# Fewer small GpSimd instructions per batch, and the two-product gate in every tile of batches 1 to 7

## The chip, the cores and the metric

The kernel runs on one core of a Trainium2 chip. A core has TensorE (PE: matmuls, with the weight loads PEld beside them), VectorE (DVE), ScalarE (ACT), GpSimd (POOL) and SyncE (SP, which here only issues transfers). Each engine works through its own queue of instructions in the order in which the program lists them. The metric is the device time of one execution in microseconds (us); lower is better.

## The reference

```python
def _attn_ref(x):                      # x: [8, 3008, 256]
    X = np.fft.fft(x, axis=1)
    X = np.fft.fft(X, axis=2)
    return X.real.astype(np.float32)

def _moe_ref(x, w_gate, w_val, w_out): # [24064, 256], [256, 1536] twice, [1536, 256]
    gate = np.maximum(x @ w_gate, 0.0)
    val = x @ w_val
    return (gate * val @ w_out).astype(np.float32)
```

The real part of a 2-D Fourier transform over sequence and channels of each of the 8 batches goes, row by row, through a gated layer with ReLU.

## The kernel before

**Transform.** Per batch, GpSimd *folds* x: it adds rows and channels to their mirror images, so that the transform over the sequence becomes products of TensorE with cosine and sine tables, and the transform over the channels is multiplied into the gate and value weights beforehand (`WA`, `WB`, and `WM`, the sine weight with the sign for the mirrored row). The folds of a batch are a list made by `fold_steps(b)`:

- six `fold_a` (L113), then the same for channel 0 in three small instructions (`fold_a0`, L116);
- `channel_128`: two small sums `c128p` (L148), and eight small scalings into `FN` (L151), the operand of the Nyquist channel;
- `load_rows` of the next batch, issued by SP;
- six `fold_pq` (L121), then `small`: six `fold_pq0` for channel 0 (L124);
- gathers of the next batch's mirrored rows (`load_mirror`, L102), interleaved with the folds into F (L128, and L132 for channel 0) and G (L137), families 1 and 0.

**Order.** The program is written out by hand. From batch 1 on, a batch is 3 blocks ("thirds") of 12 feature tiles, 36 *slots*. A slot (`slot`) lists the value products of tile k, the gate of tile k+2, the second (mirrored) half of tile k-1, a share of the output products of the block before (L496), and then some steps of other work: transform products of the next batch, 3 of them in the slots that `DFT_EVEN` and `DFT_ODD` name, and fold steps of the batch after that. Batch b transforms batch b+1 and folds batch b+2; batches 6 and 7 fold nothing. In odd batches the Nyquist products (`nyquist_steps`, L443) of two batches come after slot 18; they read `FN`, with batch b+2's part of it.

Fold steps are given out by a credit. Each step has a declared cost in us, the first number of its pair:

```python
def run_fold(us):
    credit = credit + us if todo_fold else 0
    while todo_fold and credit >= todo_fold[0][0]:
        cost, step = todo_fold.pop(0)
        step()
        credit -= cost
...
run_fold(fold_us * (1.6 if not new else .9))   # in slot; fold_us is 1.1 in batch 1, .9 after
```

`new` says that the slot builds the gate of a tile of the new kind. What is left at a batch's end is issued there at once (`run_fold(99)`). Six steps of batch 2's folds are left over for batch 1.

**Tiles.** A tile is 504 (or 497) columns of one of 12 features, with a plus and a mirrored half.

- An *old* tile (kind "o") takes its gate in three products: WA and WB, ReLU by ScalarE (L585), then WM on top and ReLU again; VectorE multiplies each by the value (L593).
- A *new* tile (kind "n") takes it in two: ScalarE seeds the bank (L684), WM gives the sine part q (L689), which ScalarE copies out (L692), WA adds the cosine part (L696). VectorE makes one argument, p - q/2 (L700, in `both`), **GpSimd adds q for the other (L701)**, and VectorE does ReLU and the multiplication in one instruction for each half (L597).

The value takes three products either way (L570, L571, L575). The L701 of tile k is listed in slot k-2 and its mult in slot k+1. In batches 1 to 5, 18 tiles are old: 6 in batch 1 and 3 in each of 2 to 5; the rest of batches 1 to 7, 234 tiles, are new. Batch 0 has another form (`first_tile`, `single_tile`), with narrower segments.

Of the kernel before, what the change touches and what calls it, by code (L numbers as in the profile page):

```python
# [13 lines left out]
ALU = mybir.AluOpType  # L14
# [18 lines left out]
def kernel(  # L33
# [8 lines left out]
    nc = tc.nc  # L42
# [18 lines left out]
    def single(name, shape, dt=F32, pool=const):  # L61
        return pool.tile(shape, dt, name=name, tag=name)
# [13 lines left out]
    XD = single("XD", [128, 2, 3, 2, D])  # L76
    XG = single("XG", [128, 2, 3, 2, D])
    PQ = single("PQ", [128, 2, 3, 2, D])

    FF = [single(f"F{i}", [128, 2, 3, 2, 129], BF16) for i in range(2)]  # L80
    GG = [single(f"G{i}", [128, 2, 3, 2, 128], BF16) for i in range(2)]
    FN = single("FN", [128, 2, 3, 2, B // 2, 2, 2], BF16)
# [6 lines left out]
    def load_rows(b, queue=None):  # L89
        o = b * S * D  # L90
        for t in range(3):
            for r in range(2):
                n = (128, 128, 120)[t]
                (queue if queue and r and t < 2 else nc.sync).dma_start(out=XD[0:n, r, t],
                                                                         in_=dram(x, o + (1 + r * H + t * 256) * D, [[2 * D, n], [D, 2], [1, D]]))

        for r in range(2):
            nc.sync.dma_start(out=XD[120:121, r, 2], in_=dram(x, o + r * H * D, [[0, 1], [0, 2], [1, D]]))

    def load_mirror(b, t, r):  # L100
        n = (128, 128, 121)[t]
        nc.gpsimd.indirect_dma_start(  # L102
            out=XG[0:n, r, t, :, :].rearrange("p a d -> p (a d)"), out_offset=None, in_=pairs,
            in_offset=bass.IndirectOffsetOnAxis(ap=gidx[0:n, 2 * t + r:2 * t + r + 1] if t < 2 else gidx2[0:n, r:r + 1], axis=0),
            element_offset=b * S * D)

    def flat(ap):
        return ap.rearrange("p t q d -> p (t q) d")
# [3 lines left out]
    def fold_a(e, p, r, t):  # L112
        e.tensor_tensor(XG[p, r, t, ::-1, 1:D], XG[p, r, t, ::-1, 1:D], XD[p, r, t, :, D - 1:0:-1], op=ALU.add)  # L113

    def fold_a0(e, p, t):
        e.tensor_tensor(XG[p, :, t, ::-1, 0], XG[p, :, t, ::-1, 0], XD[p, :, t, :, 0], op=ALU.add)  # L116

    SIGN = (ALU.add, ALU.subtract)

    def fold_pq(e, p, i, t):  # L120
        e.tensor_tensor(PQ[p, i, t, :, 1:D], XG[p, 0, t, ::-1, D - 1:0:-1], XG[p, 1, t, ::-1, 1:D], op=SIGN[i])  # L121

    def fold_pq0(e, p, i, t):
        e.tensor_tensor(PQ[p, i, t, :, 0], XG[p, 0, t, ::-1, 0], XG[p, 1, t, ::-1, 0], op=SIGN[i])  # L124

    def fold_f(e, p, ts, fam, b):
        s = flat(PQ[p, fam, ts])
        e.tensor_tensor(flat(FF[b % 2][p, fam, ts])[:, :, 1:129], s[:, :, 1:129], s[:, :, D - 1:D - 129:-1], op=ALU.add)  # L128

    def fold_f0(e, p, ts, fam, b):  # L130
        s = flat(PQ[p, fam, ts])[:, :, 0:1]
        e.tensor_tensor(flat(FF[b % 2][p, fam, ts])[:, :, 0:1], s, s, op=ALU.add)  # L132

    def fold_g(e, p, ts, fam, b):

        s = flat(PQ[p, 1 - fam, ts])
        e.tensor_tensor(flat(GG[b % 2][p, 1 - fam, ts])[:, :, 1:128], s[:, :, 1:128], s[:, :, D - 1:D - 128:-1], op=ALU.subtract)  # L137

    def fold_steps(b):

        e, p, ts = nc.gpsimd, slice(0, 128), slice(0, 3)
        steps = [(1.1, lambda r=r, t=t: fold_a(e, p, r, t)) for t in range(3) for r in range(2)]
        steps += [(0.5, lambda: [fold_a0(e, p, t) for t in range(3)])]

        def channel_128():
            for i in range(2):
                c = c128p[:, i]
                e.tensor_tensor(c, XG[:, 0, :, ::-1, 128], XG[:, 1, :, ::-1, 128], op=SIGN[i])  # L148
                for par in range(2):
                    for half in range(2):  # L150
                        e.tensor_scalar(FN[:, i, :, par, b // 2, half, b % 2], c[:, :, par], scalar1=-2.0 if par == 0 and half == i else 2.0,  # L151
                                        op0=ALU.mult, scalar2=0.0, op1=ALU.add)
        steps.append((0.5, channel_128))
        gathers = []
        if b + 1 < B:
            steps.append((0.0, lambda: load_rows(b + 1)))
            gathers = [(1.3, lambda r=r, t=t: load_mirror(b + 1, t, r)) for t in range(3) for r in range(2)]
        steps += [(1.1, lambda i=i, t=t: fold_pq(e, p, i, t)) for t in range(3) for i in range(2)]

        def small():  # L160
            for i in range(2):
                for t in range(3):
                    fold_pq0(e, p, i, t)
        steps.append((0.8, small))
        last = []
        for fam in (1, 0):
            last.append((1.7, lambda fam=fam: fold_f(e, p, ts, fam, b)))
            last.append((1.9, lambda fam=fam: (fold_f0(e, p, ts, fam, b), fold_g(e, p, ts, fam, b))))
        for k in range(6):
            steps += gathers[k:k + 1] + last[k:k + 1]  # L170
        return steps
# [3 lines left out]
    def iota(dst, pattern, base, mult):  # L175
        nc.gpsimd.iota(dst, pattern=pattern, base=base, channel_multiplier=mult, allow_small_or_imprecise_dtypes=True)
# [16 lines left out]
    dvec = single("dvec", [128, 129], pool=st_)  # L193
    go = single("go", [128, 2])
    c128p = single("c128p", [128, 2, 3, 2])

    iota(gidx[:].rearrange("p (t r) -> p t r", r=2), [[-128, 2], [-H // 2, 2]], H - 1, -1)
    iota(pidx[:], [[0, 1]], 0, 1)
# [9 lines left out]
    for r, want in enumerate((0, H // 2)):  # L208
        have = H - 1 - 256 - 120 - r * H // 2
        nc.vector.scalar_tensor_tensor(gf[:, r:r + 1], in0=z[:], scalar=float(want - have), in1=gf[:, r:r + 1],  # L210
                                       op0=ALU.mult, op1=ALU.add)
# [48 lines left out]
    for n, c in enumerate(order):  # L260
        q, m = (single(f"{s}{c}", [128, NJ], pool=st_) for s in "qm")
# [41 lines left out]
    for t in range(3):  # L303
        p, ts = slice(0, ROWS[1][t]), slice(t, t + 1)
# [12 lines left out]
    for p, ts in ((slice(0, 128), slice(0, 2)), (slice(0, ROWS[1][2]), slice(2, 3))):  # L317
        for part in (fold_f, fold_f0, fold_g):
            part(nc.gpsimd, p, ts, 0, 0)
    iota(kvec[:, 0:NE], [[2, NE]], 0, 0)  # L320
    start_pool.__exit__(None, None, None)
    ch128 = nc.dram_tensor("ch128", (B, 4 * NJ + 1), BF16, kind="Internal").ap()
    b2 = single("b2", [128, NF])
# [292 lines left out]
    def tile_of(block, fi, uvc):  # L616
        c0, n = block[:2]
        cols = slice(c0, c0 + n)
        return {"n": n, "fi": fi, "f": slice(fi * 128, (fi + 1) * 128), "us": uvc[0][:, cols], "vs": uvc[1][:, cols], "c": uvc[2][:, cols]}
# [45 lines left out]
    def new_tiles():  # L665
        for b in range(1, B):
            for blk, block in enumerate(thirds):
                for fi in range(NF):
                    st = tile_of(block, fi, uv[b])
                    st["kind"] = "o" if b < 6 and fi % (6 if b < 2 else 12) == 5 else "n"  # L670
                    yield st

    def prime():
# [5 lines left out]
    def seed(st, p=None):  # L679

        if st is None or st["kind"] == "o":
            return
        st["p"] = p or bank("p")
        nc.scalar.activation(st["p"][:, 0:st["n"]], st["c"], ACTF.Copy, scale=b2[:, st["fi"]:st["fi"] + 1])  # L684

    def sine_part(st):
        n = st["n"]
        st["g"] = bank("g")
        nc.tensor.matmul(st["g"][:, 0:n], lhsT=WM[0][:, st["f"]], rhs=st["vs"], start=True, stop=True)  # L689
        q = space()  # L690
        st["s"] = q, space(), q
        nc.scalar.copy(q[:, 0:n], st["g"][:, 0:n])  # L692

    def cosine_part(st):
        n = st["n"]
        nc.tensor.matmul(st["p"][:, 0:n], lhsT=WA[0][:, st["f"]], rhs=st["us"], start=False, stop=True, skip_group_check=True)  # L696

    def both(st):
        n, (q, sp, sm) = st["n"], st["s"]
        nc.vector.scalar_tensor_tensor(sp[:, 0:n], in0=q[:, 0:n], scalar=-0.5, in1=st["p"][:, 0:n], op0=ALU.mult, op1=ALU.add)  # L700
        nc.gpsimd.tensor_tensor(sm[:, 0:n], sp[:, 0:n], q[:, 0:n], op=ALU.add)  # L701
# [40 lines left out]

    uv = {0: (U, V, CB)}
    tiles, ahead = new_tiles(), []

    for b in range(B):
        blocks = thirds if b else segments
        more_b = {} if b else more
        if 0 < b < B - 2:
            todo_fold += fold_steps(b + 2)  # L750
        for blk, block in enumerate(blocks):
# [3 lines left out]
            if b == 0 and blk > 1:  # L755
                todo_fold = fold_steps(blk - 1)
                later = todo_fold[-6:] if blk == 3 else []
                del todo_fold[len(todo_fold) - len(later):]
                run_fold(99)
                todo_fold = later  # L760
            if blk == (0 if b else 2) and b + 1 < B:
# [4 lines left out]
                steps, todo_dft = todo_dft, []  # L766
# [20 lines left out]
            if (b, blk) == (0, 0):  # L787
                for fi in range(NF):
                    st = tile_of(block, fi, (U, V, CB))
# [4 lines left out]
            elif not paired:  # L794
                for fi in range(NF):
                    st = tile_of(block, fi, (U, V, CB))
                    add_h(st, hs)
                    tag = {(3, 8): "g", (3, 9): "d", (3, 10): "g", (3, 11): "d"}.get((blk, fi), "p")
                    last = []
                    if (blk, fi) == (3, 11):  # L800
                        last = [lambda: (sine_part(ahead[1]), cosine_part(ahead[1]), both(ahead[1]), seed(ahead[2]))]
# [54 lines left out]
```

## Time and profile before

| What | Value |
|---|---|
| median of 3 runs | 647.6 us (647.58 to 647.83) |
| profiled execution: span, first to last instruction | 646.1 us |
| what the median has beyond the span | 1.5 us |
| busy: PE / DVE / ACT / POOL | 96% / 84% / 70% / 83% |
| granted TensorE clock | 1.00 |
| batch 1 from, to | 114.0, 189.4 us |
| batches 2 to 5, each | 74.2 to 75.3 us |
| batch 6 | 73.6 us |
| POOL L701, 504 columns | 1.25 us each, 234 of them |
| POOL small instructions (L116, L124, L132, L148, L151) | 0.20 to 0.23 us each |

A row of a group names line, engine, operation and operands, then busy time, mean duration and the idle time ahead. A stretch row gives the busy microseconds of PE, PEld, DVE, ACT and POOL with the number of instructions, then the granted clock, the DMA share and GB/s. A waits row says who waited for whom, the total, the number of times and the longest. The chain of waits is followed back from the end of its window: at each step to what released an instruction, or to the one before it on its engine. A batch's bounds are read from the first value product (L570) of its slot 0. The profiled execution is a single one; its span is compared with the median by the 1.5 us between them.

### The profile page before, as it was taken

The numbers are of one execution on the slowest core, as the hardware profiler recorded it, in microseconds if no ns is written. First come the engines' busy times: TensorE is split into PE (matmuls) and PEld (weight loads), VectorE is DVE, ScalarE is ACT, GpSimd is POOL, SyncE is SP. The second block draws the span as 40 slices with busy tenths as digits, with TensorE's granted clock in tenths as the row PEclk, the third lists the DMA queues.
The fourth block names the chain that finished last, engine by engine and source line by source line (L and its number), as shares of the span: only waits on it lengthen the run. The fifth ranks groups of instructions, "written<-read, shape, count | busy, mean of one in ns | idle before, by whom it ended". The sixth has DMA issues, their size and how long they took to land.

```text
span 646.1 us, 12223 instructions
## 1 busy us (share of the span) xinstructions
PE 620.9 (96%) x4160; PEld 401.6 (62%) x4160; DVE 543.7 (84%) x970; ACT 450.6 (70%) x822; POOL 535.5 (83%) x593
## 2 busy tenths in 40 slices
PE   0999999999999999999999999999999999999996
PEld 0356676566666666666666666666666666666665
DVE  8875566887888899898998889988899899999990
ACT  8697666767666776777677677676777767777751
POOL 8589997899999999999899999999876656666660
PEclk9999999999999999999999999999999999999999
DMA  8922544224332433241222422311211111111112
GB/s 227 207 67 64 178 127 137 62 68 145 89 83 63 127 98 90 64 136 58 89 84 78 129 73 82 93 35 49 73 34 49 44 62 49 35 48 49 50 49 79
DMA packets 42438, 55.24 MB, mean 85 GB/s; under 512 B 5153, under 2 KB 32353, under 8 KB 42376
## 3 DMA queue, kind: packets, MB, share of 16 engines
q1 hardware_dynamic: 34552, 39.23, 19.7%
q0 software_dynamic: 7536, 14.72, 9.3%
q8 instruction: 32, 0.52, 0.4%
q10 hardware_dynamic: 288, 0.52, 0.2%
q14 instruction: 30, 0.25, 0.1%
HBM read 32.14 MB, written 24.67 MB: 88 GB/s over the span
## 4 chain that ended last, share of the span: by engine, by line
PE 69%; DVE 12%; POOL 9%; issue 6%; ACT 3%; DMA 0%; DVEq 0%; SPq 0%; ACTq 0%; POOLq 0%
PE o L496 27%; PE v L575 7%; PE v L570 7%; PE v L571 7%; DVE h L597 6%; PE g L689 5%; PE p L696 5%; DVE r L700 5%; POOL r L701 4%; PE d L385 4%; PE p L575 1%; POOL XG L113 1%; POOL PQ L121 1%; POOL XG L102 1%; PE p L571 1%
## 5 line engine op out<-in xcount | busy, mean ns | idle before, releaser
L701 POOL TENSOR_TENSOR r<-r 128x504 f32<-128x504 f32 (+1 forms) x234 | 291.7, 1252 | 73.8 <-DVE r L700 72.3
L496 PE MATMUL o<-wo,h 128*128 128x256 bf16 x2304 | 342.3, 273 | 0.0
L597 DVE SCALAR_TENSOR_TENSOR h<-r,v 128x504 bf16<-128x504 f32 (+1 forms) x468 | 297.3, 673 | 51.1 <-PE v L575 37.8
L496 PEld LDWEIGHTS <-h 128*128 128x128 bf16 x2304 | 225.2, 98 | 114.7 <-issue 2.3
L684 ACT ACTIVATE p<-CB,b 128x504 f32<-128x504 bf16 (+1 forms) x234 | 160.0, 684 | 55.3 <-DVE r L700 52.8
L692 ACT COPY r<-g 128x504 f32<-128x504 f32 (+1 forms) x234 | 135.0, 577 | 58.6 <-PE g L689 54.5
L700 DVE SCALAR_TENSOR_TENSOR r<-r,p 128x504 f32<-128x504 f32 (+1 forms) x234 | 156.7, 670 | 0.6 <-ACT r L692 0.6
L575 PE MATMUL v<-V,WM 128*128 128x504 bf16 (+3 forms) x296 | 108.6, 367 | 1.6 <-DVE h L597 1.0
L570 PE MATMUL v<-U,WA 128*128 128x504 bf16 (+3 forms) x296 | 108.6, 367 | 0.1
L571 PE MATMUL v<-V,WB 128*128 128x504 bf16 (+3 forms) x296 | 108.7, 367 | 0.0
L593 DVE TENSOR_TENSOR h<-r,v 128x376 bf16<-128x376 f32 (+3 forms) x124 | 68.9, 580 | 25.7 <-PE v L575 13.6
L689 PE MATMUL g<-V,WM 128*128 128x504 bf16 (+1 forms) x234 | 87.8, 375 | 0.5 <-ACT r L692 0.3
L696 PE MATMUL p<-U,WA 128*128 128x504 bf16 (+1 forms) x234 | 87.8, 375 | 0.0
L502 ACT COPY os<-o 128x512 f32<-128x512 f32 x96 | 55.7, 580 | 14.5 <-PE o L496 8.1
L570 PEld LDWEIGHTS <-WA 128*128 128x128 bf16 x366 | 35.7, 98 | 38.3 <-issue 8.9
L571 PEld LDWEIGHTS <-WB 128*128 128x128 bf16 x366 | 35.7, 98 | 35.7 <-ACT WB L291 0.7
L102 POOL DMA_INDIRECT XG<-in_x_dram,gidx x48 | 48.8, 1017 | 8.7 <-issue 6.3
L113 POOL TENSOR_TENSOR XG<-XG,XD 128x510 f32<-128x510 f32 x42 | 52.5, 1265 | 0.1
L585 ACT ACTIVATE r<-g 128x504 f32<-128x504 f32 (+3 forms) x48 | 27.3, 569 | 35.0 <-PE g L571 31.8
L585 ACT ACTIVATE r<-p 128x376 f32<-128x376 f32 (+1 forms) x80 | 38.2, 490 | 18.7 <-PE p L575 10.9
L121 POOL TENSOR_TENSOR PQ<-XG 128x510 f32<-128x510 f32 x42 | 45.0, 1091 | 0.0
L575 PEld LDWEIGHTS <-WM 128*128 128x128 bf16 x366 | 35.8, 98 | 11.4 <-issue 0.2
(127 smaller groups left out, 430.4 us busy)
## 6 DMA issues: line engine op xcount, KB each, us to landing
out_dram<-os SPq DMA_DIRECT2D x118, 128.0 KB
XD<-in_x_dram SPq DMA_DIRECT2D x30, 256.0 KB
out_dram<-os SPq DMA_DIRECT2D x62, 120.0 KB
XD<-in_x_dram SPq DMA_DIRECT2D x16, 240.0 KB
CB<-ch SPq DMA_DIRECT2D x7, 376.2 KB
out_dram<-os SPq DMA_DIRECT2D x10, 127.0 KB
XG<-in_x_dram,gidx POOLq DMA_INDIRECT x48
h<-in_moe_w_gate_dram POOLq DMA_DIRECT2D x3, 256.0 KB
```

Of the source, the lines that this page charges most:

```text
L496: nc.tensor.matmul(st["p"][:, q, :], lhsT=hs[f][:, sign, h0:h0 + 128], rhs=wo[:, f, :], start=(f == 0), stop=(f == NF - 1))
L570: nc.tensor.matmul(bank[:, 0:st["n"]], lhsT=WA[i][:, st["f"]], rhs=st["us"], start=True, stop=False)
L571: nc.tensor.matmul(bank[:, 0:st["n"]], lhsT=WB[i][:, st["f"]], rhs=st["vs"], start=False, stop=True)
L575: nc.tensor.matmul(bank[:, 0:st["n"]], lhsT=WM[i][:, st["f"]], rhs=st["vs"], start=False, stop=True, skip_group_check=True)
L593: nc.vector.tensor_tensor(half_h(st, sign), (r or st["r"])[:, 0:n], st["v"][:, 0:n], op=ALU.mult)
L597: nc.vector.scalar_tensor_tensor(half_h(st, sign), in0=st["s"][1 + sign][:, 0:n], scalar=0.0, in1=st["v"][:, 0:n], op0=ALU.max, op1=ALU.mult)
L684: nc.scalar.activation(st["p"][:, 0:st["n"]], st["c"], ACTF.Copy, scale=b2[:, st["fi"]:st["fi"] + 1])
L689: nc.tensor.matmul(st["g"][:, 0:n], lhsT=WM[0][:, st["f"]], rhs=st["vs"], start=True, stop=True)
L692: nc.scalar.copy(q[:, 0:n], st["g"][:, 0:n])
L696: nc.tensor.matmul(st["p"][:, 0:n], lhsT=WA[0][:, st["f"]], rhs=st["us"], start=False, stop=True, skip_group_check=True)
L700: nc.vector.scalar_tensor_tensor(sp[:, 0:n], in0=q[:, 0:n], scalar=-0.5, in1=st["p"][:, 0:n], op0=ALU.mult, op1=ALU.add)
L701: nc.gpsimd.tensor_tensor(sm[:, 0:n], sp[:, 0:n], q[:, 0:n], op=ALU.add)
```

## The change

Three small instructions of `fold_a0` become one; the eight scalings into `FN` become one product of a broadcast `c128p` with a constant tile `sg` of +2 and -2, which three memsets at the start fill; the six of `fold_pq0` become two; the two of `fold_f0` become one, which moves from the last steps into `small`, ahead of the F folds. That is 19 into 5, and the declared costs follow. Every tile of batches 1 to 7 gets the kind "n".

```diff
-        steps += [(0.5, lambda: [fold_a0(e, p, t) for t in range(3)])]
+        steps += [(0.2, lambda: e.tensor_tensor(XG[:, :, :, ::-1, 0], XG[:, :, :, ::-1, 0], XD[:, :, :, :, 0], op=ALU.add))]
 
         def channel_128():
             for i in range(2):
-                c = c128p[:, i]
-                e.tensor_tensor(c, XG[:, 0, :, ::-1, 128], XG[:, 1, :, ::-1, 128], op=SIGN[i])
-                for par in range(2):
-                    for half in range(2):
-                        e.tensor_scalar(FN[:, i, :, par, b // 2, half, b % 2], c[:, :, par], scalar1=-2.0 if par == 0 and half == i else 2.0,
-                                        op0=ALU.mult, scalar2=0.0, op1=ALU.add)
+                e.tensor_tensor(c128p[:, i], XG[:, 0, :, ::-1, 128], XG[:, 1, :, ::-1, 128], op=SIGN[i])
+            e.tensor_tensor(FN[:, :, :, :, b // 2, :, b % 2].rearrange("p i t q h -> p i (t q) h"),
+                            c128p[:].rearrange("p i t q -> p i (t q)").unsqueeze(3).to_broadcast([128, 2, 6, 2]), sg[:], op=ALU.mult)
         steps.append((0.5, channel_128))
...
         def small():
             for i in range(2):
-                for t in range(3):
-                    fold_pq0(e, p, i, t)
-        steps.append((0.8, small))
+                e.tensor_tensor(PQ[:, i, :, :, 0], XG[:, 0, :, ::-1, 0], XG[:, 1, :, ::-1, 0], op=SIGN[i])
+            zero = PQ[:, :, :, :, 0:1].rearrange("p i t q d -> p (i t q) d")
+            e.tensor_tensor(FF[b % 2][:, :, :, :, 0:1].rearrange("p i t q d -> p (i t q) d"), zero, zero, op=ALU.add)
+        steps.append((0.6, small))
         last = []
         for fam in (1, 0):
             last.append((1.7, lambda fam=fam: fold_f(e, p, ts, fam, b)))
-            last.append((1.9, lambda fam=fam: (fold_f0(e, p, ts, fam, b), fold_g(e, p, ts, fam, b))))
+            last.append((1.7, lambda fam=fam: fold_g(e, p, ts, fam, b)))
...
+    sg = single("sg", [128, 2, 6, 2])
...
     iota(kvec[:, 0:NE], [[2, NE]], 0, 0)
+    nc.gpsimd.memset(sg[:], 2.0)
+    for i in range(2):
+        nc.gpsimd.memset(sg[:, i, 0::2, i:i + 1], -2.0)
...
-                    st["kind"] = "o" if b < 6 and fi % (6 if b < 2 else 12) == 5 else "n"
+                    st["kind"] = "n"
```

## The prediction

> **What bounds the kernel now.** I read the page first, then the waits, then the chain of waits window by window, then GpSimd's timeline. The page's whole-run rows say "TensorE, 96% busy", but the chain has 9% of POOL and 12% of DVE in it, so I looked where those lie. The waits view, largest first, with the two rows that concern the sum of a new tile that GpSimd forms (L701) and the mult that reads it (L597):
>
> ```profile
> POOL r L701 <- DVE r L700: 72.3, 101, 3.8
> ...
> DVE h L597 <- POOL r L701: 4.4, 7, 1.1
> ```
>
> GpSimd mostly waits for VectorE, so over the whole run it has room. But VectorE also waited for GpSimd, 7 times. The chain of waits of the stretch 118 to 200 us (start, us, what) shows where:
>
> ```profile
> 126.58 1.25 POOL r L701
> ...
> 149.33 0.48 POOL XG L116 x3
> 149.81 0.16 POOL c128p L148
> 149.97 0.08 issue
> 150.05 0.68 POOL FN L151 x4
> 150.73 0.17 POOL c128p L148
> 150.90 0.08 issue
> 150.98 0.68 POOL FN L151 x4
> 151.65 1.04 POOL PQ L121
> ...
> 186.00 0.04 DVE h L597
> ```
>
> From 126.58 to 186.00 us, nearly all of batch 1 (its slot 0 is at 114.0, batch 2's at 189.4), the chain stays on GpSimd. The stretches (PE, PEld, DVE, ACT, POOL busy) of batch 1, of batch 4 (three old tiles) and of batch 6 (no old tile, no folds):
>
> ```profile
> 126.00:186.00 60.00, 59.93 (x396) 37.84 (x396) 50.34 (x87) 41.45 (x74) 58.41 (x68) 1.00 0.35 99
> 338.90:413.10 74.20, 74.20 (x497) 48.42 (x496) 66.36 (x114) 52.54 (x92) 70.71 (x77) 1.00 0.29 90
> 488.40:562.00 73.60, 73.60 (x494) 48.07 (x493) 67.75 (x117) 53.14 (x92) 45.01 (x36) 1.00 0.16 48
> ```
>
> In batch 1 POOL and PE are both full (58.41 of 60, the rest being gaps ahead of gathers); in batch 4 only PE is, POOL having 3.49 us over. Putting each L701 beside its L597 mult: in batch 1 the sum ends 2.5 to 3 us ahead of its use at first, 0.2 us for tile 16 (use at 149.56), 0.03 for tiles 26, 30, 32, 33 and 37 (194.08, use 194.11); tile 38 (batch 2, tile 2) ends at 195.28 and is used at 196.49, 1.2 us to spare. GpSimd's backlog is thus at its limit through the second half of batch 1. All at granted clock 1.00.
>
> **1. Tiles to two gate products (18 tiles: 6 in batch 1, 3 each in 2 to 5).** TensorE: a product less per tile. Batch 6 against batch 4 is this very change: (74.20 - 73.60) / 3 = 0.20 us per tile. VectorE: (67.75 - 66.36) / 3 = 0.46 us more per tile, hidden in 5.85 us idle that batch 6 keeps; uncovered it would be 8.3. ScalarE: (53.14 - 52.54) / 3 = 0.2, hidden in 20 us idle (3.6 otherwise). GpSimd: one L701 more per tile. Its cost in a full queue is the start-to-start spacing, 1.21 us:
>
> ```profile
> 145.65 1.25 POOL L701 TENSOR_TENSOR r<-r 128x504 f32<-128x504 f32 x1
> 146.86 1.26 POOL L113 TENSOR_TENSOR XG<-XG,XD 128x510 f32<-128x510 f32 x1
> 148.09 1.25 POOL L701 TENSOR_TENSOR r<-r 128x504 f32<-128x504 f32 x1
> 149.30 0.51 POOL L116 TENSOR_TENSOR XG<-XG,XD 128x4 f32<-128x4 f32 x3
> 149.77 0.20 POOL L148 TENSOR_TENSOR c128p<-XG 128x6 f32<-128x6 f32 x1
> ```
>
> **2. The merged instructions.** The same timeline gives the old price by spacing: channel 0 and channel 128 from 149.30 to 151.61, 2.31 us; the six L124 0.93 (163.94 to 164.87); two L132 at 0.155, 0.31. Sum 3.55. New: 0.17 (12 elements in one), two L148 0.31 with one gap of 0.09 and one product of 24 elements, 0.20 to 0.30, then two L124 of 6 elements, a gap, and the zero column, 0.5: about 1.37. The trace has no such 24-element instruction; small ones of 2, 3, 4 and 6 elements last 201, 202, 206 and 204 ns, so elements are nearly free. Bounds: 0.9 (no element, no gap costs) to 2.4 (three times the product, and waits). Saved: 2.2 per batch, bounds 1.2 to 2.6. "Perfetto Trace Analysis" of the Trainium skill (GPSIMD Engine Instruction) says to time GpSimd by the spacing of starts, since its reported spans are unreliable; the trace agrees (spans of 0.20, spacing of 0.155). By spans (19 x 0.20 less 5 x 0.22) the saving would be 2.7 and the time 0.5 us less than I forecast.
>
> Where no one waits, this is worth nothing: in batch 0 the folds of batches 1 and 2 end 2.2 us sooner, but GpSimd then idles 3.8 us before tile 0's L701, and TensorE reads batch 1's folds 3 us after they end. The three memsets of `sg` (0.11 each by the other memsets) stand at 27 us ahead of the even tables, whose first row ends at 32.4 and is read at 35.2; cover gone they cost 0.3.
>
> **3. The order of folds.** GpSimd's fold steps are issued by a credit per slot: 1.1 x 0.9 = 0.99 in batch 1, 1.1 x 1.6 = 1.76 in a slot that builds an old tile. Before: 30 x 0.99 + 6 x 1.76 = 40.3 for steps declared at 38.8 (8.8 left of batch 2, 30.0 of batch 3); all are out by slot 34. After: 36 x 0.99 = 35.6 for 8.6 + 29.1 = 37.7. The last two gathers don't fit and are flushed after slot 35, ahead of tile 38's L701. `channel_128` needs credit 15.9: reached in slot 16 (16.8), behind tile 18's L701, where it was in slot 15 ahead of it. From batch 2 on 36 x 0.81 = 29.16 just holds 29.1. The gathers' readers come some 10 us later; SP's x loads, and the output stores behind them, wait for the fold steps up to 3 us longer, covered by four `os` buffers of which one is taken per three slots (6 us). The zero column moves ahead of the F fold, where nobody waits for it.
>
> **The sum in batch 1.** (a) FN. TensorE's Nyquist products start at 151.97, right when the last FN write is done (151.65). After: the queue ahead of it gains four L701 (tiles 5, 11, 17, 18), 4.84 us, and loses 0.30 + 1.14 + 0.15 = 1.6 of merges: FN at about 154.5 to 154.9. TensorE, in order, stands there for some 2.6 to 3.3 us with all of slot 19 behind it. (b) Tile 38. Ahead of it are six L701 more, 7.26, less 2.18 (batch 3) and 0.15 (batch 2's last L132): 4.9 us later, with 1.2 to spare: 3.7 us lost. (a) and (b) are one delay of one queue, not to be added: by tile 38 the program is 3.7 us behind its old time, and the product saved on the six tiles is swallowed.
>
> **The sum behind it.** Batch 4's GpSimd after: 70.71 + 3 x 1.21 - 2.18 = 72.2 of 73.6 us: 1.4 over, so TensorE is the bound again and the 11 remaining tiles (53 to 173; 41 still lies under the delay) give 11 x 0.20 = 2.2. Total +3.7 - 2.2 = +1.5. The profiled span 646.1 becomes 647.6; the median stands 1.5 above the span (647.6), so 649.1.
>
> **Rivals.**
> A, the delay persists (chance 0.18): the 24-element product with its gap costs 1.0 more than priced. Batch 1 loses 1.0 more, the 1.4 us over in an even batch shrinks to 0.4, the backlog doesn't drain, and half of the 2.2 isn't earned: 649.1 + 1.0 + 1.1 = 651.2. For: no row of that form. Against: flat cost of small rows.
> B, a wash (0.17): the merges save the upper bound, 2.6, and VectorE, whose idle was 0.52 us ahead of tile 38's mult, swallows part: 3.7 - 0.4 - 0.5 - 2.2 = +0.6, 648.2.
> C, faster (0.15): GpSimd's backlog doesn't reach TensorE, since the two-buffer `v` banks let it run on. Then 18 x 0.20 = 3.6 are saved: 644.0. It decides if sums may be 4.9 - 1.2 us later than now without a wait. For: TensorE's own idle in batch 1 is under 0.6 us. Against: the mults at 0.03 us spare, and slots of 2.2 and 2.4 us late in batch 1 where 1.92 is the rule.
> That the tiles are not converted can be ruled out: each "n" tile of batch 6 shows the new form.
>
> **How the numbers follow.** The forecast case has 0.50, its own range 648.2 to 650.3 from the merge bounds (+1.0, -0.4) and the spare time. A median can tell about 0.2%, 1.3 us, from no change: the bounds are 646.3 and 648.9. Slower: A and two thirds of the forecast case and a little of B, 0.53. Same: the rest of the forecast case and most of B, 0.31. Faster: C and a remainder, 0.16. The range leaves out most of C and the tail of A: 646.8 to 651.3.
>
> **What would show it.** A wait of TensorE for POOL's FN of 2.6 us or more in batch 1 (about 152 to 155); the chain on POOL from about 120 to 200 us; L597 waiting for L701 early in batch 2; L701 x252; merged rows near 0.2 us; batch 4 at 73.6 us with some 1.4 us of POOL idle. I am wrong if TensorE's slots in batch 1 come out at the old spacing or shorter, or if POOL idles in batch 1.

## The result, and the profile after

The changed kernel takes 652.74 us (median of 4; 652.02 to 654.64) against 647.72 before: a ratio of 1.0083, 95% interval 1.0068 to 1.0098. It is slower, as forecast, but by 5.0 us where 1.5 was forecast, and outside the range. A second set of five executions, on one chip with runs 2, 3 and 6 below, gave 652.05 (ratio 1.0073, 1.0060 to 1.0087).

Lines move by two: the sum of a new tile is now L703, its mult L599, the Nyquist products L445, the write of FN L148, the mirrored value product L577. The waits of the profiled execution (span 652.4 us):

```profile
DVE h L599 <- POOL r L703: 5.7, 6, 3.0
...
PE d L445 <- POOL FN L148: 3.3, 1, 3.3
PE v L577 <- DVE h L599: 3.1, 4, 2.1
```

Two single waits carry nearly all of it: TensorE stands 3.3 us for FN, and 2.1 us for a mult of VectorE, which itself waited 3.0 us for an L703. These are places (a) and (b) of the prediction. Then come stretches, with the columns of the table before; the seventh is the granted clock:

```profile
126.00:186.00 60.00, 56.58 (x359) 35.02 (x358) 49.08 (x85) 39.12 (x68) 56.10 (x53) 0.94 0.30 93
186.00:240.00 54.00, 51.86 (x336) 33.24 (x334) 45.67 (x79) 36.37 (x63) 52.96 (x51) 0.97 0.29 88
346.30:419.90 73.60, 73.60 (x493) 48.10 (x492) 67.76 (x117) 53.19 (x92) 71.68 (x66) 1.00 0.30 90
```

Batch 4 (last row) runs as forecast, 73.60 us with 71.68 of POOL. In the two stretches with the waits the clock isn't 1.00. TensorE's timeline behind the first wait (start us, us, line, operation; the bracket is the idle time ahead):

```profile
154.87 2.05 PE L445 MATMUL d<-tabC,FN 128*4 128x377 bf16 x12 [3.27 <-POOL FN L148]
156.85 0.60 PE L691 MATMUL g<-V,WM 128*128 128x504 bf16 x1
...
159.15 0.63 PE L572 MATMUL v<-U,WA 128*128 128x504 bf16 x1
159.57 0.63 PE L573 MATMUL v<-V,WB 128*128 128x504 bf16 x1
...
161.74 0.38 PE L577 MATMUL v<-V,WM 128*128 128x504 bf16 x1
161.95 0.38 PE L572 MATMUL v<-U,WA 128*128 128x504 bf16 x1
```

The same 504-column product starts 0.42 us after the one before it at 159, and 0.21 us at 161.7. The trace's clock record has half clock from 154.07 for 6.83 us and from 205.27 for 3.41 us, behind the two waits. That isn't in the prediction at all.

### The profile page after: what moved, and what is told of

It reads as the page before. It is cut to its first block, busy times and chain, and to the rows that moved or that the text cites. A ratio compares the mean times of both kernels' runs of the same rounds, so it can differ in the third digit from the quotient of the medians.

```text
span 652.4 us, 12167 instructions
## 1 busy us (share of the span) xinstructions
PE 621.8 (95%) x4140; PEld 401.4 (62%) x4142; DVE 553.1 (85%) x988; ACT 455.3 (70%) x822; POOL 542.0 (83%) x516
## 4 chain that ended last, share of the span: by engine, by line
PE 67%; DVE 13%; POOL 9%; issue 7%; ACT 3%; DMA 0%; DVEq 0%; SPq 0%; ACTq 0%; POOLq 0%
PE o L498 27%; PE v L577 7%; DVE h L599 7%; PE v L572 6%; PE v L573 6%; PE g L691 6%; PE p L698 5%; POOL r L703 5%; DVE r L702 5%; PE d L387 3%; POOL XG L102 1%; PE p L577 1%; POOL XG L113 1%; PE p L573 1%; PE p L572 1%
## 5 line engine op out<-in xcount | busy, mean ns | idle before, releaser
L703 POOL TENSOR_TENSOR r<-r 128x504 f32<-128x504 f32 (+1 forms) x252 | 313.2, 1251 | 73.7 <-DVE r L702 72.6
L599 DVE SCALAR_TENSOR_TENSOR h<-r,v 128x504 bf16<-128x504 f32 (+1 forms) x504 | 318.6, 673 | 51.4 <-PE v L577 34.4
L498 PE MATMUL o<-wo,h 128*128 128x256 bf16 x2304 | 347.0, 273 | 0.0
L686 ACT ACTIVATE p<-CB,b 128x504 f32<-128x504 bf16 (+1 forms) x252 | 172.4, 684 | 74.1 <-DVE r L702 72.3
L694 ACT COPY r<-g 128x504 f32<-128x504 f32 (+1 forms) x252 | 145.6, 578 | 76.6 <-PE g L691 72.0
L702 DVE SCALAR_TENSOR_TENSOR r<-r,p 128x504 f32<-128x504 f32 (+1 forms) x252 | 168.8, 670 | 0.6 <-ACT r L694 0.6
L577 PE MATMUL v<-V,WM 128*128 128x504 bf16 (+3 forms) x296 | 109.1, 368 | 3.7 <-DVE h L599 3.1
L691 PE MATMUL g<-V,WM 128*128 128x504 bf16 (+1 forms) x252 | 95.2, 378 | 0.4 <-ACT r L694 0.3
L698 PE MATMUL p<-U,WA 128*128 128x504 bf16 (+1 forms) x252 | 95.0, 377 | 0.0
L595 DVE TENSOR_TENSOR h<-r,v 128x376 bf16<-128x376 f32 (+1 forms) x88 | 44.7, 543 | 25.6 <-PE v L577 13.6
L587 ACT ACTIVATE r<-p 128x376 f32<-128x376 f32 (+1 forms) x80 | 38.3, 490 | 18.6 <-PE p L577 11.4
L577 PEld LDWEIGHTS <-WM 128*128 128x128 bf16 x348 | 34.1, 98 | 7.7 <-issue 0.2
L691 PEld LDWEIGHTS <-WM 128*128 128x128 bf16 x252 | 24.8, 98 | 6.8 <-issue 1.3
```

The source lines that it names most:

```text
L498: nc.tensor.matmul(st["p"][:, q, :], lhsT=hs[f][:, sign, h0:h0 + 128], rhs=wo[:, f, :], start=(f == 0), stop=(f == NF - 1))
L577: nc.tensor.matmul(bank[:, 0:st["n"]], lhsT=WM[i][:, st["f"]], rhs=st["vs"], start=False, stop=True, skip_group_check=True)
L599: nc.vector.scalar_tensor_tensor(half_h(st, sign), in0=st["s"][1 + sign][:, 0:n], scalar=0.0, in1=st["v"][:, 0:n], op0=ALU.max, op1=ALU.mult)
```

## The experiments

Two theories. **Clock**: the waits are those of the queue sum, and what is missing is that TensorE, having stood idle, works on at half clock. **Waits alone**: the clock row is incidental, GpSimd's queue is longer than I summed.

**1. The changed kernel again, five executions.**

> Two theories. CLOCK: beside its waits for GpSimd, TensorE loses 1.7 us for every 3.41 us stretch at half clock that follows such a wait, so the executions of one kernel differ by how many stretches they have. Expected: mean clock 0.997 goes with about 652.1, 0.994 with 653.3, 0.992 with 654.6, on one line with some 0.2 us of scatter. WAITS ALONE: the half clock is incidental, GpSimd's queue is simply longer than summed; then time and mean clock of an execution need not go together, and all executions lie within 0.3 us of each other.

| mean clock | time of each execution, us (both sets) |
|---|---|
| 1.000 | 650.03 |
| 0.997 | 651.93, 652.02, 652.05, 652.26 |
| 0.994 to 0.995 | 653.20, 653.22, 653.22 |
| 0.992 | 654.64 |

Time goes with clock, in steps of 2.0, 1.2 and 1.4 us; one program differs by 4.6 us between executions. The execution with a full clock was the one profiled here (span 647.8). It has the same wait, and then:

```profile
154.58 1.13 PE L445 MATMUL d<-tabC,FN 128*4 128x377 bf16 x12 [3.27 <-POOL FN L148]
155.64 0.39 PE L691 MATMUL g<-V,WM 128*128 128x504 bf16 x1
...
156.83 0.38 PE L572 MATMUL v<-U,WA 128*128 128x504 bf16 x1
157.05 0.38 PE L573 MATMUL v<-V,WB 128*128 128x504 bf16 x1
```

An equal idle time of 3.27 us thus brings half clock in one execution and none in another. The clock record shows what differs: the clock changes only whole multiples of 3.41 us after its first change (20.95 + 39 x 3.413 = 154.07), and these times fall differently in each execution. In the halved one, 2.47 us of the wait (151.60 to 154.87) lie in one such stretch, 150.65 to 154.07. In the other, a boundary at 152.80 (19.68 + 39 x 3.413) cuts the wait (151.31 to 154.58) into 1.49 and 1.78 us.

**2. Spare products in the first wait.**

```diff
+    def fill(n):
+        g = bank("g")
+        for _ in range(n):
+            nc.tensor.matmul(g[:, 0:504], lhsT=WA[0][:, 0:128], rhs=uv[1][0][:, 0:504], start=True, stop=True)
...
+            if g == 1:
+                fill(14)
             d = psD.tile([128, 512], F32, name="d", tag="d")
```

> Fourteen spare products of 504 columns (2.98 us, results unused) are listed ahead of batch 1's Nyquist products, where TensorE stood idle for 3.27 us. CLOCK: the Nyquist products still start near 154.9, but at full clock, and slots 18 to 20 take 6.3 to 7.3 us less the wait, about 3.0 us less than the 8.47 + 2.80 us of before; GpSimd's idle behind the wait (2.7 us) goes, so tile 38's L701 ends near 200.5 instead of 203.2; a wait of 2 to 3 us and one half-clock stretch stay there. Time 649.9 to 651.2. WAITS ALONE: TensorE gets nothing from spare work: 652.0 to 653.3, as the changed kernel.

Measured 650.05 us (ratio 1.0040, 1.0026 to 1.0053); four executions at 650.03 to 650.06, one at 651.51 with a clock of 0.997. TensorE's timeline:

```profile
151.17 3.14 PE L587 MATMUL g<-U,WA 128*128 128x504 bf16 x14
154.61 1.13 PE L447 MATMUL d<-tabC,FN 128*4 128x377 bf16 x12 [0.30 <-POOL FN L148]
```

FN comes as late as ever (154.61). Giving TensorE 3 us more to do, whose results nobody reads, makes the program 2 us faster. Waits alone falls.

**3. Spare products in both waits** (the same, and `if cur["at"] == 40: fill(9)` behind `seed(after)`, slot 4 of batch 2).

> As the run with spare products ahead of the Nyquist products, and nine more (1.9 us) in slot 4 of batch 2, where TensorE waited 2.14 us behind tile 38's L701. CLOCK: mean clock 1.000, no half-clock stretch inside the program; every execution within 0.3 us; 1.7 us less than with the first fill alone: 648.2 to 649.7. WAITS ALONE: 652.0 to 653.3.

650.15 us, all five between 650.08 and 650.26, clock 1.000 each time. The spread is gone. The median lies above the expected 648.2 to 649.7: I had counted on 1.7 us less than run 2, but by the mean clock the second wait had brought half clock in only one of that run's five. At full clock the changed kernel thus takes 650.0 to 650.3 us in all of runs 1 to 3.

**4. The two parts alone.** The merged instructions, with the old tiles kept:

```diff
-                    st["kind"] = "n"
+                    st["kind"] = "o" if b < 6 and fi % (6 if b < 2 else 12) == 5 else "n"
```

> The merged instructions and their declared costs alone; the 18 old tiles stay old. CLOCK and the queue sum: GpSimd gets 2.2 us per batch back and nobody else any work, so only what batch 1 lost to GpSimd before comes back, up to 0.8 us in its third block; everywhere else TensorE is the bound and nothing changes. Time 646.7 to 647.6, no half clock. If the merged instructions had a price of their own (a wait, a slow form) it would show here as slower than 648.

646.74 us (ratio 0.9985, 0.9976 to 0.9994), about 1 us faster. Batch 1's third block takes 23.56 us instead of 24.38: the 0.8 us that it had lost to GpSimd. The new tiles, with the old small instructions (the kernel before with `st["kind"] = "n"`):

> All tiles of batches 1 to 7 new, the small instructions as before. GpSimd then has 2.2 us more per batch than in the changed kernel: in batches 2, 4 it needs 70.7 + 3.6 = 74.3 us where TensorE needs 73.6, so the queue sum sees waits in each of batches 2 to 5 too: FN some 4.5 to 5 us late in batch 1, tile 38 some 3 to 4, then about 1 us per batch: 8 to 9 us of waits net of the products saved, 655.5 to 657 at full clock. CLOCK adds 3 to 6 us for the stretches behind the two long waits: 658 to 662. WAITS ALONE stays at 655.5 to 657.

659.32 us (ratio 1.0183, 1.0167 to 1.0199): 658.14 and 658.35 at clock 0.996, 660.28 and 660.46 at 0.988. The waits have grown as the queue sum has it, and now TensorE also waits about 0.6 us once in each of batches 2, 3 and 5:

```profile
DVE h L597 <- POOL r L701: 13.8, 23, 3.9
...
PE v L575 <- DVE h L597: 6.7, 9, 3.5
...
PE d L443 <- POOL FN L151: 4.1, 2, 3.5
```

The parts don't add (-1.2 and +11.4 against +4.3 to +5.0 together): 2.2 us of GpSimd per batch are worth 1 us in all where little waits for it, and 7 where TensorE does.

**5. Is it one delay or two losses?** Nyquist products listed later:

```diff
-    DFT_ODD = (3, 0, 3, 0, 0, 0) * 3 + (1, 0, 3, 0, 3, 0, 0) + (0,) * 11
+    DFT_ODD = (3, 0, 3, 0, 0, 0) * 3 + (0, 0, 0, 1, 3, 0, 3) + (0,) * 11
```

> The changed kernel with batch 1's (and 3's and 5's) Nyquist products listed three slots later, and the six transform products behind them one or two slots later. The prediction called the late FN and the late tile 38 one delay of one queue. ONE DELAY: the wait ahead of the Nyquist products goes (under 0.5 us), but GpSimd's queue still sets the end of tile 38's L701 at about 200.1 us, with waits of VectorE for L701 spread before it: at full clock the same span of 647.8, time 650.0, and one half-clock stretch less at most, 650.0 to 651.6. TWO LOSSES: the 3.3 us of the first wait are saved, 646.5 to 647.5.

652.91 us (ratio 1.0079, 1.0066 to 1.0093): neither range. The chain of waits up to tile 38's L703, here and in run 1's execution at full clock:

```profile
194.80 0.74 POOL G L137
195.54 1.21 issue
196.75 0.60 POOL XG L102
197.34 0.74 issue
198.09 1.03 POOL XG L102
199.11 0.03 issue
199.14 1.27 POOL r L703
...
201.75 0.37 PE v L577
```

```profile
194.47 0.75 POOL G L137
...
198.81 1.27 POOL r L703
...
201.42 0.37 PE v L577
```

The wait for FN is gone, and TensorE comes out behind tile 38 at 201.75 instead of 201.42: a second loss of 3.3 us that could be saved does not exist. It is one delay of one queue, the G and the two flushed gathers standing right ahead of the L703. The half clock behind the 2.29 us wait there, in all five executions by their mean clock (0.996 or 0.997), was in the range. What lies above it is the edit's own: it puts transform products straight behind the Nyquist products, whose bank ScalarE has yet to empty (three waits of 0.45 us), and batches 3 and 5 take 0.6 us longer each than in run 1.

**6. Old tiles in batch 1 alone.**

```diff
-                    st["kind"] = "n"
+                    st["kind"] = "o" if b < 2 and fi % 6 == 5 else "n"
```

> The merged instructions stay, batch 1 keeps its six old tiles, batches 2 to 5 have the new form alone. Both theories put the loss into batch 1: GpSimd has 2.3 us less there than in the kernel before, no wait over 0.5 us, clock 1.000; batch 1 gains up to 0.8 us that late slots lost to GpSimd, and the twelve tiles give 2.3: 644.2 to 645.3. A rival, GpSimd too full in batches 2 to 5 as well, would give 647 or more, with waits for L701 there.

645.02 us (ratio 0.9964, 0.9952 to 0.9976), clock 0.999 to 1.000; five of six executions lie between 644.97 and 645.63, one took 647.26 at full clock, which I can't explain. The change is a gain in batches 2 to 5 and a loss in batch 1 only.

**7. GpSimd's queue shortened by what batch 0 can take.** The left-over steps of batch 2's folds, six in the changed kernel, cut to four and to two, the last also with a slower credit:

```diff
-                later = todo_fold[-6:] if blk == 3 else []
+                later = todo_fold[-4:] if blk == 3 else []    # run "later4"
+                later = todo_fold[-2:] if blk == 3 else []    # runs "later2", "later2_pace"
...
-                    pending = slot(cur, *ahead, per_tile, 1.1 if b == 1 else .9)
+                    pending = slot(cur, *ahead, per_tile, 1.0 if b == 1 else .9)    # "later2_pace"
```

> The changed kernel with two of batch 2's six left-over fold steps (a gather and an F, 3.0 us) done in batch 0. GpSimd's queue in batch 1 is still full, but 3.0 us shorter: FN arrives at about 151.7, when TensorE comes for it, and tile 38's L701 some 3 us sooner; what is lost is spread over a dozen waits of 0.2 to 0.6 us each. QUEUE SUM: 2.4 us less than the changed kernel at full clock (650.05), 647.2 to 648.2. CLOCK: with no wait over 0.7 us the clock stays at 1.000 and all executions lie within 0.5 us of each other; if half-clock stretches come from GpSimd's backlog as such and not from long idle times of TensorE, they show here too (over 649).

647.53 us (ratio 0.9999, 0.9990 to 1.0008): 2.5 us less than the changed kernel at full clock. The clock is 0.999 or 1.000 in all eleven executions, though they spread over 0.7 us (647.37 to 648.11), not the 0.5 expected. Here a backlog in small waits costs its own time and no more.

> The changed kernel with four of the six fold steps of batch 2 that batch 0 leaves to batch 1 (a gather, an F, a gather, a G: 6.0 us of GpSimd) done in batch 0, where GpSimd idles about 6 us ahead of tile 0's L701. Batch 1's queue then has 4.9 - 6.0 = 1.1 us less than in the kernel before. No wait for FN or L701 over 0.5 us, clock 1.000; batch 1 earns its six products as well: some 0.5 to 1.2 us below the run whose batch 1 kept its old tiles (645.0): 643.8 to 644.8. Rival: batch 0 or the first slots of batch 1 wait for the 6 us moved there, 645 or more.

646.90 us (ratio 0.9984, 0.9975 to 0.9993): the rival's side. Batch 1's blocks take 24.13, 26.74 and 25.24 us: the first slots don't wait, the last block does (six waits of L599 for L703, 3.0 us; in the whole program ten, 5.8 us). I had counted the work taken out of batch 1 and not the credit: without the four steps, the credit of 0.99 hands out batch 3's folds earlier, faster than GpSimd can work.

> The run with four fold steps moved to batch 0, with batch 1's credit cut from 0.99 to 0.90 per slot (fold_us 1.1 to 1.0): with 31.7 declared, 0.99 gives the steps out by slot 31, ahead of what GpSimd can do in that time (70.6 us of work against 66.3 of slots: 4.3 us behind, 3.3 is what a tile allows), 0.90 by slot 35 (75.5 against 74.0). QUEUE SUM: the waits of 0.3 us late in batch 1 shrink to 0.6 us in all, 2.6 us less than that run (646.9): 643.7 to 645.0, the fastest of all; clock 1.000. Rival: the waits come from somewhere else (VectorE's own queue) and the pace changes nothing: 646.5 to 647.

644.25 us (ratio 0.9950, 0.9936 to 0.9964), the fastest of all. Its waits and stretches:

```profile
DVE h L599 <- POOL r L703: 1.2, 2, 0.6
```

```profile
126.00:186.00 60.00, 59.85 (x402) 38.20 (x401) 54.83 (x95) 43.74 (x76) 59.13 (x55) 1.00 0.32 94
186.00:240.00 54.00, 54.00 (x362) 35.14 (x360) 49.07 (x87) 39.08 (x70) 53.11 (x52) 1.00 0.30 89
```

GpSimd is as full as before (59.13 of 60), but its steps come in step with TensorE, which is full as well.

## Why the prediction was right in its sign and wrong in its size

**The queue sum held.** FN was forecast at 154.5 to 154.9 us and came at 154.83; TensorE's wait at 2.6 to 3.3, it was 3.27. Tile 38 was forecast to put the program 3.7 us behind; its mult starts 3.6 us later, at 200.10 in the execution at full clock against 196.49 before. The two rows, before and at full clock:

```profile
196.49 1.27 DVE L597 SCALAR_TENSOR_TENSOR h<-r,v 128x504 bf16<-128x504 f32 x2 [0.52 <-POOL r L701]
```

```profile
200.10 1.27 DVE L599 SCALAR_TENSOR_TENSOR h<-r,v 128x504 bf16<-128x504 f32 x2 [3.01 <-POOL r L703]
```

Behind it the products saved were put at 2.2 us: from there to the end takes 447.7 us against 449.6, 1.9 less. The span at full clock is 647.8; the working gave 647.6. Part 1's 0.20 us per tile held in batch 4 (73.60), and its cover on VectorE and ScalarE too; batches 3 and 5 gained only 0.3 and 0.5 us for their three tiles. The merged instructions last 0.22 to 0.25 us each, and by the spacing of starts they save 2.1 us per batch (0.28, 1.21 and 0.61; forecast 2.2).

**What failed is the step from the waits to the time.** The working of "by tile 38 the program is 3.7 us behind its old time" took a TensorE that works on after a wait as it did before. It doesn't: behind the two long waits its clock halves, in all but one of nine executions, for one, two or three stretches of 3.41 us, and while TensorE is the bound such a stretch costs about half its length, 1.7 us, less what of it falls into idle time (6.83 us from 154.07 hold 0.8 of idle: 3.0 lost; 3.41 from 205.27: 1.7). In the profiled execution that makes 4.7 of the 4.8 us between its span, 652.4, and the forecast's 647.6. The median, 652.74, lies 3.6 us above the forecast's 649.1: 2.7 of it is half clock (against 650.03 at full clock), 0.7 the time outside the span (below), 0.2 the sum. The prediction had written "all at granted clock 1.00" of the kernel before and had not asked what keeps it there. The kernel before has no idle time of TensorE over 0.7 us between 17 us and its last product at 641.8, so that record says nothing of a wait amid the work. But its start shows the price, in two rows that the prediction did not use:

```profile
16.01 1.03 PE L290 MATMUL v<-h,TA 128*128 128x512 bf16 x2 [16.01 <-ACT TA L279]
...
25.80 0.59 PE L290 MATMUL o<-h,TA 128*128 128x512 bf16 x2
```

Behind the first wait, of 16 us, two products take 1.03 us, and two of the same size 0.59 later; the clock record turns to full in between, at 21.18. "TensorE: Matmul & The Clock Gate" of the Trainium skill (Part 1, and the table under Why this matters for your kernels) bears on just this step: it warns of idle gaps over about 3 us between bursts of matmuls, and has half clock follow an idle window of about 3.4 us and full clock a busy one. The traces agree on the half and on the length, 3.41 us. On the threshold they differ: 2.14 and 2.29 us were enough in some executions, and 3.27 was not in one.

**A smaller miss** is the 1.5 us added to the span. In the changed kernel the time is 2.2 us above the span, in the kernel before 1.75 by the later runs, which list both for each execution. So some 0.25 us come from setting one execution's span against the median of three (646.1 and 1.75 make the slowest of them, 647.83), and 0.45 us are new time outside the program's first and last instruction. Run 6 and both runs of 4 have 1.75, all others 2.2. I did not find the cause.

**The rivals.** A, the delay that persists, did not occur: batch 4 keeps 1.9 us of POOL idle (forecast 1.4); with the old small instructions it does occur (run 4). B, a wash, gave the merges 2.6 us, and they are worth 2.1. C, a TensorE that runs on, is refuted by the 3.27 us.

## What to carry to other kernels

When a sum ends in "the engine then stands still for 3 us", the price of TensorE's idle time is not only its length: read what clock it resumes with, and if the profile at hand has no idle time of that length, put it down as a term with bounds (here 0 to 3.0 us behind a wait of 3.3 us, 0 to 1.7 behind one of 2.1), not at nothing. In these runs one wait of 3 us could cost what many short ones didn't, so a late queue was better spread than bunched. And where steps are handed out by a credit, moving work elsewhere changes the pace of what is left: set the two together.

## What the runs showed of the hardware

The granted clock takes two values here, full and half. Amid the program half clock lasts 3.41 us or twice that in the traces, and in each of the twelve the clock changes on a grid of 3.41 us, whose place differs from one execution to the next. It followed idle times of TensorE of 2.1 to 3.5 us amid otherwise dense work, not every time: of ten executions whose one long wait was 2.1 to 2.3 us (runs 2 and 5), six had a half-clock stretch by their mean clock.

What went with it in the traces, worked out from TensorE's timelines, is how much of the idle time fell into one stretch of the grid. Half clock began four times amid the program, each time right behind a stretch with 2.14 to 2.47 us of idle time; the other stretches up to the last product had at most 1.8 us, and none was followed by half clock. In run 4's trace, for one, a wait of 3.45 us was cut into two such parts and brought none. Where between 1.8 and 2.1 us the border lies, and why half clock lasted two stretches behind the first wait, no run shows; none moved the grid on purpose either. Spare products into a bank that nobody reads kept the clock up in all five executions of run 3.
